# Pair-wise token mixing, two more pairs turned by the DMA crossbar behind held loads, and a shorter mask chain, in a block-sparse attention and mixer kernel on one core

## The chip, the cores and the metric

The kernel runs on one core of a Trainium2 chip. The metric is the device time of one execution in microseconds; the figure for a kernel is the median over its runs. Profiles come from one profiled execution, whose span (first to last instruction of the program) is a little shorter than its time.

The engines are named as in the profile: PE is TensorE (PEld its weight loads), DVE VectorE, ACT ScalarE, POOL GpSimd, SP the engine that issues most of the stores and the crossbar transposes.

## The reference

Inputs are q, k and v of shape (4 batches, 8 heads, 768 rows, 64), a table of three sampled key blocks for each of the 24 query blocks (a block is 32 rows), and four mixer weights. All arrays but the table are float32; the output is (4, 768, 512) in float32.

```python
scores = (q @ k.transpose(0, 1, 3, 2)) / np.sqrt(64)
# a key block is allowed when it neighbours the query block (distance <= 1),
# when either block is the first or the last, or when it is sampled for that query block
scores = np.where(mask, scores, -1e9)
attn = softmax(scores)
x = (attn @ v).transpose(0, 2, 1, 3).reshape(4, 768, 512)

h  = np.maximum(x.transpose(0, 2, 1) @ w_tok1, 0) @ w_tok2     # 768 -> 256 -> 768, over the rows
u  = x + h.transpose(0, 2, 1)
out = u + np.maximum(u @ w_ch1, 0) @ w_ch2                     # 512 -> 1536 -> 512, over the channels
```

## The kernel before

**Units of work.** Two heads make a pair; there are 16 pairs (`p`), four to a batch (`b`). The scores of a pair are made in nine visits (`t`, `jj`), each of four matmuls into one PSUM tile `ps`: 256 keys by 256 queries for both heads. ACT takes the exponential of a visit (`et`, L686), and PE multiplies `et` by v (`po`, L762, eight matmuls of 65 columns; column 65 sums the weights). DVE divides (L776, L777) and writes `x` of the batch, which the mixer reads.

**The mask.** For pairs 0 to 3 the mask goes into the score matmul as 24 more contraction rows (88 rows instead of 64), for one head at a time. For pairs 4 to 15 the two heads of a pair lie in the two halves of the contraction rows (64 rows each), two matmuls run side by side, and DVE multiplies `et` by a 0/1 mask (L694). Such visits go to PE two at a time. The rows of the mask are made at the start by a chain of small DVE operations (L353 to L375) from three GpSimd iotas and the sampled table; a matmul `pm_e` (L410) and copies (L417) bring them into `qtb[0]`.

**Turning k and q.** The score matmul needs k and q with the head dimension on partitions (`ktb`, `qtb`, four buffers each, pair p in buffer p % 4). For pairs below `NPE = 8`, PE turns them against an identity matrix (L618, `tk` and `tq`, 12 matmuls a pair) and DVE or ACT copies the result out of PSUM (L632, L647). From pair 8 on, SP issues two DMA transposes a pair (L587, the crossbar), from `klay` and `qlay`, which a DVE copy (L565) fills. The copies of these pairs are planned after the last load has landed (`all_loaded`).

**The loads.** k, q and v of a pair, as bfloat16, are three DMAs of GpSimd (L254); the queue goes on in the order of `loads`: pairs 4 to 15, with the channel weights (L273, L280) after pairs 5 and 7 and parts of the mask copies (L532) after pairs 5 to 7. A load waits for a free home (`homes`, which include unused halves of `ktb` and `qtb`).

**The mixer.** Token mixing of a batch is `tok(b, g)`, for the two halves `g` (two pairs each): 12 matmuls of 256 columns (`pm_tok`, L842), a ReLU (`a_t`), 12 of 256 columns (L867), and three DVE additions into `x` (L875). The result must be turned for the channel mixing (`uT`): for batch 0 on PE (`pm_ut`, L896, 12 matmuls for each half), for the others by SP's crossbar (L820). Channel mixing of a batch, `ch(b)`, is 24 groups of four matmuls of 384 columns (L934) with ReLUs on ACT or DVE (L804, L806), and then 6 groups of 12 matmuls of 512 columns (L960), DVE additions (L972) and stores by SP.

**The order.** A planner in the kernel's Python writes out the order of every engine's instructions ahead of time. It holds streams of PE work by priority (0 for scores, 1 for `po`, 2 for turning pairs, 0.5 for token mixing of batch 0, 3 for that of the others, 4 for channel mixing), a cost for each piece, due times for loads, and the number of buffers (`ps` 2, `pm` 3, `et` 7). At each planned moment the stream with the smallest number that is ready goes. ACT takes other work only when no exponential is pending. On the chip each engine then works strictly in this order, and waits where data is not there.

One detail of that order: the first channel matmuls of a group ask only for their own part of `uT`,

```python
yield 162.5, [st[b]["uT_there"][dmc], ch1_there[dmc]], tags, emit, ...
```

so that two of the four matmuls of the first group stand in PE's program as soon as half `g = 0` is mixed, and hold one of the three `pm` buffers until half `g = 1` is done.

Of the kernel before, what the change touches and what calls it, by code (L numbers as in the profile page):

```python
# [174 lines left out]
def kernel(  # L175
# [22 lines left out]
    NET = 7  # L198
    NPE = 8
    NT0 = 4  # L200
# [25 lines left out]
    def landing(issue, nbytes):  # L226
        dma["free"] = max(dma["free"], issue + 3.2 * US) + nbytes / RATE
        return Ev(dma["free"] + 0.15 * US)

# [31 lines left out]
    def load_tok(t):  # L261
        nc.gpsimd.dma_start(
            out=w_tok1[:, :, :], in_=APx(moe_w_tok1, 0, [[NC * DT, 128], [1, NC * DT]])
        )
        tok1_there.t = landing(t, S * DT * 2).t
        nc.gpsimd.dma_start(
            out=w_tok2[:, :, :, :], in_=APx(moe_w_tok2, 0, [[S, 128], [128 * S, 2], [1, S]])
        )
        tok2_raw.t = landing(t, S * DT * 2).t
# [50 lines left out]

    for i in range(8):
        idle_mm()
    nc.gpsimd.iota(dki[R, :], pattern=[[1, 24]], base=0, channel_multiplier=-1)
    nc.gpsimd.iota(qbi[R, :], pattern=[[0, 1]], base=0, channel_multiplier=1)
# [26 lines left out]
    t2add = sb1.tile([128, 24], BF16, name="t2add")  # L351

    nc.vector.tensor_copy(out=dkf[R, :], in_=dki[R, :])  # L353
    nc.vector.tensor_copy(out=edge[R, :], in_=qbi[R, :])
    nc.vector.tensor_tensor(out=dkf[R, :], in0=dkf[R, :], in1=dkf[R, :], op=ALU.mult)
    nc.vector.tensor_scalar(
        out=edge[R, :], in0=edge[R, :], scalar1=-11.5, scalar2=None, op0=ALU.add
    )
    nc.vector.tensor_tensor(out=edge[R, :], in0=edge[R, :], in1=edge[R, :], op=ALU.mult)
    nc.vector.tensor_scalar(  # L360
        out=edge[R, :], in0=edge[R, :], scalar1=121.0, scalar2=None, op0=ALU.is_gt
    )
    nc.vector.tensor_scalar(
        out=bandg[R, :], in0=dkf[R, :], scalar1=1.0, scalar2=edge[R, 0:1],
        op0=ALU.is_le, op1=ALU.max,
# [50 lines left out]
    def e2_copy(copy, hf, hd, t):  # L416
        copy(out=qtb[0][R, hd, 384 * hf : 384 * hf + 384], in_=t[R, 0:384])  # L417
# [3 lines left out]
    qt0 = first_turn("q", 0)  # L421
    first_lay(acopy, "k", 0)
    kt0 = first_turn("k", 0)
    e2a, e2b = e2_mm(0, psM, "pm"), e2_mm(0, psO, "po")
    for i in range(4):
        idle_mm()
    first_evac(acopy, "q", 0, 0, qt0)
    first_evac(acopy, "q", 0, 1, qt0)
    e2_copy(acopy, 0, 0, e2a)
    first_evac(vcopy, "k", 0, 0, kt0)  # L430
    first_evac(vcopy, "k", 0, 1, kt0)
    e2_copy(vcopy, 0, 1, e2b)
    first_lay(acopy, "k", 1)
    first_lay(vcopy, "q", 1)
    START = 6.3 * US
    P.now = START
    for eng in P.free_at:
        P.free_at[eng] = START
    P.free_at["dve"] = START + 550.0
    f_there = {("k", 0): Ev(START), ("q", 0): Ev(START), ("k", 1): Ev(), ("q", 1): Ev()}  # L440

# [109 lines left out]
    copied = {}  # L551
    all_loaded = Ev()

    def relayout(p):
        lays = {}
        for nm in ("k", "q", "v") if p else ("v",):
# [18 lines left out]
            if nm != "v" and p >= NPE:  # L575
                deps.append(all_loaded)
            lays[nm + "ev"] = P.op(("dve",), {"dve": 320.0}, deps, emit, prio=2 if nm != "v" else 3)
# [76 lines left out]
    def alias(a, b):  # L654
        a.same_as = b
# [48 lines left out]
    def qk_deps(p, t, jj):  # L704
# [4 lines left out]
        return deps + [rows_there[0]] * (t > 0)  # L709

    def qk_stream():
        todo = list(steps)
        while todo:
# [12 lines left out]

            s2 = todo.pop(0)
            yield lambda p=s2[0]: (p, 1) in qT_there
            evs = [Ev(), Ev()], [Ev(), Ev()]

            def emit(s=s, s2=s2, evs=evs):
                scores(s, evs[0][0], evs[1][0])
                scores(s2, evs[0][1], evs[1][1])
                evs[0][0].t = P.now + 330.0 + P.PE_LAT + P.SEM
                evs[0][1].t = P.now + 560.0 + P.PE_LAT + P.SEM

            yield 650.0, qk_deps(*s) + qk_deps(*s2), [("ps", 2), ("et", 2)], emit, None
            for x, ev in zip((s, s2), evs[0]):
                if x[1:] == (2, 2):
                    alias(qk_done[x[0]], ev)  # L740

# [54 lines left out]

    st = {}

# [31 lines left out]
    def tok(b, g):  # L830
        deps = [x_there[2 * g + 4 * b + i, h] for i in range(2) for h in range(3)] + [tok1_there]

        urgent = 0.5 if b == 0 else 3
        box = {}
# [18 lines left out]
        a_t = sbw.tile([128, 2, 256], BF16, tag="a_t", name=f"a_t{b}_{g}")  # L853
        a_there = relu_op(lambda: a_t[:, :, :], box["pm"][:, :, :], [last], urgent)
        alias(rel, a_there)
        u_evs = []
        for s2 in range(3):
# [21 lines left out]

            ev = P.op(("dve",), {"dve": 695.0}, [last], add, prio=urgent)  # L880
            alias(rel, ev)
            u_evs.append(ev)
        alias(a_rel, last)
        if b > 0:
            turn_by_crossbar(b, g, u_evs)
            return
        for dmc in (2 * g, 2 * g + 1):
            last, rel, tbox = Ev(), Ev(), {}
            for sc in range(NC):
                def emit(sc=sc, dmc=dmc, rel=rel, tbox=tbox):  # L890
                    if sc == 0:
                        if dmc == 0:
                            new_uT(b)
                        P.take("pm", rel)
                        tbox["pt"] = psM.tile([128, NC, 128], BF16, tag="pm", name=f"pm_ut_{b}_{dmc}")
# [4 lines left out]
                    )  # L900
                tags = [("pm", 1)] if sc == 0 else []
                if sc == 0 and dmc == 0:
                    tags.append(("uT", 1))
                yield 56.0, [u_evs[sc // 2]], tags, emit, last if sc == NC - 1 else None

# [6 lines left out]

            ev = P.op(("dve", "act"), {"dve": 555.0, "act": 740.0}, [last], evac, prio=urgent)
            alias(rel, ev)
            alias(st[b]["uT_there"][dmc], ev)

    def ch(b, pool, tag):
# [4 lines left out]
        for cc in range(12):  # L922
            for sh in range(2):
                last, rel, pbox = Ev(), Ev(), {}
                for dmc in range(4):
# [14 lines left out]
                    if first and cc == 0 and sh == 0:  # L940
                        tags.append(("rc", 1))
                    yield 162.5, [st[b]["uT_there"][dmc], ch1_there[dmc]], tags, emit, last if dmc == 3 else None
                ev = relu_op(
# [9 lines left out]
        for sc, lo, n in parts:  # L953
# [12 lines left out]
            def fin(eng, sc=sc, lo=lo, n=n, pbox=pbox):  # L966
# [10 lines left out]
                else:  # L977
# [4 lines left out]
                    )  # L982
                nc.sync.dma_start(
                    out=APx(out, b * S * DM + sc * DM + lo, [[NC * DM, 128], [1, n]]),
                    in_=o[:, 0:n],
                )

# [11 lines left out]

    def tok_stream(bs):  # L1000
        for b in bs:
            for g in range(2):
                yield from tok(b, g)

    def ch_stream():
# [5 lines left out]
    P.stream(2, tr_stream())  # L1011
    P.stream(0.5, tok_stream((0,)))
    P.stream(3, tok_stream((1, 2, 3)))
    P.stream(4, ch_stream())
    P.stream(1.8, mask_stream())


    loads = deque()
    for p in range(4, NP):
# [5 lines left out]
        if 5 <= p <= 7:  # L1025
            loads.append(spread_mask(p - 5))


# [9 lines left out]
    def pull():  # L1038
        while loads:
            x = loads[0]  # L1040
            if callable(x):
                if maskb_there.t is None:
                    return
                x(max(P.now, maskb_there.t))
            else:
# [6 lines left out]
                t, home = min(free_from)  # L1052
                load_pair(x, t, home)
                tenant[home] = x
                if x == NP - 1:
                    all_loaded.t = arrive["v", x].t
            loads.popleft()
# [36 lines left out]
```

The softmax here doesn't subtract the row's maximum and nothing guards it: scores larger than these inputs give would overflow.

## Time and profile before

| | |
|---|---|
| median of 7 runs (lowest to highest) | 257.35 us (256.69 to 257.98) |
| profiled execution: time, span | 256.69 us, 254.8 us |
| PE busy | 247.4 us, 2738 matmuls in the records |
| DVE busy | 180.3 us |
| ACT busy | 173.9 us, 139.0 of it in 144 exponentials |
| POOL busy | 49.1 us |
| DMA | 26.35 MB, 103 GB/s on average |
| exponentials of pair 0, pair 4, pair 8, pair 15 begin at | 7.42, 43.83, 94.78, 180.60 us |

The profiled execution is the fastest of the seven and lies 0.66 us under the median; 1.89 us of it lie outside the span. Busy times of PE count each matmul from its issue to its modelled end, so a chain of short matmuls reads as one busy stretch; what PE really spends is read from the distance between starts. Some matmul records are missing from the trace (2738 of 2757).

### The profile page before, as it was taken

To read this page: it belongs to the slowest core of one execution; us is meant where nothing else is said; L and a number is where in the kernel's file an instruction comes from. 1 tells how busy PE (TensorE), PEld (TensorE's weight loads), DVE (VectorE), ACT (ScalarE), POOL (GpSimd) and SP (SyncE) were. 2 spreads that over 40 slices of the span, in tenths; PEclk is the share of its full clock that TensorE was granted. 3 is DMA by queue.
4 is the path that set the end of the run, shared out by engine and by line. 5 is a ranking of instruction groups with operands and counts; after the bars stand their busy time and mean duration, and the time that the engine had idled before them with its cause. 6 is when DMAs were issued, how large, how long until landed. Compare 5 with 4: busy or idle time off the path is not lost.

```text
span 254.8 us, 6559 instructions
## 1 busy us (share of the span) xinstructions
PE 247.4 (97%) x2738; PEld 158.8 (62%) x2757; DVE 180.3 (71%) x397; ACT 173.9 (68%) x215; POOL 49.1 (19%) x84
## 2 busy tenths in 40 slices
PE   8899999999999999999999999999999999999995
PEld 3588888766566557555666566557567744565444
DVE  7987678898899889889989898988986313200222
ACT  5899999988787677678888767767776510277100
POOL 8846969477300000000000000000000000000000
PEclk9999999999999999999999999999999999999999
DMA  6999999999976342294043311411610222300122
GB/s 154 189 216 202 212 202 206 204 201 201 202 130 102 74 115 73 59 151 106 0 59 68 64 42 26 122 44 41 59 46 4 43 63 84 124 0 3 41 110 96
DMA packets 42461, 26.35 MB, mean 103 GB/s; under 512 B 23680, under 2 KB 38800, under 8 KB 42432
## 3 DMA queue, kind: packets, MB, share of 16 engines
q0 software_dynamic: 15104, 12.98, 32.1%
q1 hardware_dynamic: 27056, 12.76, 21.4%
q8 instruction: 21, 0.34, 0.5%
q10 hardware_dynamic: 272, 0.20, 0.3%
q14 instruction: 8, 0.07, 0.1%
HBM read 26.74 MB, written 6.29 MB: 130 GB/s over the span
## 4 chain that ended last, share of the span: by engine, by line
PE 88%; ACT 6%; DVE 3%; issue 2%; ACTq 0%
PE pm_ch L934 25%; PE pm_ch L960 24%; PE ps L676 15%; PE po L762 12%; ACT et L686 6%; PE pm_tok L867 4%; PE pm_tok L842 4%; PE ps_idle L316 2%; DVE x L875 1%; DVE et L694 1%; PE pm_ut L896 1%; DVE qtb L417 0%; PE tk L618 0%; PE pm_e L410 0%; PE tq L618 0%
## 5 line engine op out<-in xcount | busy, mean ns | idle before, releaser
L686 ACT ACTIVATE et<-ps 128x1024 bf16<-128x1024 f32 x144 | 139.0, 1024 | 33.1 <-PE ps L676 32.6
L934 PE MATMUL pm_ch<-uT,w_ch 128*128 128x384 bf16 x384 | 73.3, 326 | 0.1
L694 DVE TENSOR_TENSOR et<-et,mask 128x1024 bf16<-128x1024 bf16 x108 | 70.0, 684 | 1.7 <-ACT et L686 1.7
L960 PE MATMUL pm_ch<-w_ch,rc 128*128 128x512 bf16 (+2 forms) x293 | 68.3, 362 | 1.2 <-issue 0.3
L762 PEld LDWEIGHTS <-et 128*128 128x128 bf16 x1152 | 48.5, 97 | 17.7 <-issue 2.4
L676 PE MATMUL ps<-qtb,ktb 64*128 64x256 bf16 (+1 forms) x576 | 54.7, 272 | 1.3 <-ACT et L686 0.9
L762 PE MATMUL po<-vaug,et 128*128 128x65 bf16 x1152 | 54.9, 193 | 0.4 <-DVE x L777 0.2
L934 PEld LDWEIGHTS <-w_ch 128*128 128x128 bf16 x384 | 34.0, 97 | 20.9 <-issue 3.1
L972 DVE TENSOR_TENSOR o<-pm_ch,x 128x512 f32<-128x512 f32 x23 | 15.8, 687 | 41.0 <-PE pm_ch L960 41.0
L804 ACT ACTIVATE rc<-pm_ch 128x384 bf16<-128x384 f32 x56 | 27.5, 491 | 24.9 <-PE pm_ch L934 24.6
L676 PEld LDWEIGHTS <-ktb 64*128 64x128 bf16 (+1 forms) x576 | 29.3, 95 | 20.6 <-issue 15.6
L960 PEld LDWEIGHTS <-rc 128*128 128x128 bf16 x312 | 26.8, 97 | 24.1 <-issue 2.5
L806 DVE TENSOR_SCALAR rc<-pm_ch 128x384 bf16<-128x384 f32 x40 | 22.0, 555 | 5.7 <-PE pm_ch L934 5.0
L777 DVE TENSOR_TENSOR x<-po,recip 128x256 bf16<-128x256 f32 x48 | 20.4, 425 | 1.7
L875 DVE TENSOR_TENSOR x<-pm_tok,x 128x512 bf16<-128x512 f32 x24 | 16.0, 686 | 2.7 <-PE pm_tok L867 2.6
L776 DVE RECIPROCAL recip<-po 128x4 f32<-128x4 f32 x48 | 8.7, 181 | 12.9 <-PE po L762 12.4
L867 PE MATMUL pm_tok<-a_t,w_tok 128*128 128x256 bf16 x96 | 13.5, 275 | 0.1
L842 PE MATMUL pm_tok<-x,w_tok 128*128 128x256 bf16 x96 | 12.5, 273 | 0.0
L867 PEld LDWEIGHTS <-w_tok 128*128 128x128 bf16 x96 | 10.3, 127 | 1.6 <-issue 0.8
L842 PEld LDWEIGHTS <-w_tok 128*128 128x128 bf16 x96 | 8.9, 98 | 1.9 <-issue 0.8
L254 POOL DMA_DIRECT2D vraw<-in_v_dram x10 | 7.4, 739 | 2.4 <-DVE vaug L562 0.9
L532 POOL COPY mask<-maskb 128x240 bf16<-128x240 bf16 (+1 forms) x18 | 7.3, 482 | 0.0
(96 smaller groups left out, 114.9 us busy)
## 6 DMA issues: line engine op xcount, KB each, us to landing
out_dram<-o SPq DMA_DIRECT2D x23, 256.0 KB, 2.2
w_ch<-in_moe_w_ch_dram POOLq DMA_DIRECT2D x8, 384.0 KB, 10.3
vraw<-in_v_dram POOLq DMA_DIRECT2D x10, 192.0 KB, 7.6
kraw<-in_k_dram POOLq DMA_DIRECT2D x9, 192.0 KB, 9.4
qraw<-in_q_dram POOLq DMA_DIRECT2D x9, 192.0 KB, 7.9
w_tok<-in_moe_w_tok_dram POOLq DMA_DIRECT2D x2, 384.0 KB, 9.4
ktb<-in_v_dram POOLq DMA_DIRECT2D x3, 192.0 KB, 7.3
kf<-in_k_dram SPq DMA_DIRECT2D x2, 192.0 KB, 3.1
```

The lines of the kernel that those rows point to most:

```text
L676: nc.tensor.matmul(out=ps[:, hd, 256 * i : 256 * i + 256], lhsT=ktb[n][rows, h, 256 * jj + 128 * i : 256 * jj + 128 * i + 128], rhs=qtb[n] ...
L686: nc.scalar.activation(out=et[:, :, :], in_=ps[:, :, :], func=AF.Exp, scale=0.125)
L694: nc.vector.tensor_tensor(out=ets[s][:, :, :].rearrange("k h (i q) -> k h i q", i=2), in0=ets[s][:, :, :].rearrange("k h (i q) -> k h i q" ...
L762: nc.tensor.matmul(out=po[:, hd, c, :], lhsT=et[:, hd, 256 * i + 128 * c : 256 * i + 128 * c + 128], rhs=va[:, hd, 2 * jj + i, 0:65], star ...
L777: nc.vector.tensor_tensor(out=free(xs[b][:, pb // 2, 2 * t, 128 * (pb % 2) : 128 * (pb % 2) + 128], 0, [[64, 2], [256, 2], [1, 64]],), in0 ...
L804: nc.scalar.activation(out=o(), in_=i, func=AF.Relu)
L806: nc.vector.tensor_scalar(out=o(), in0=i, scalar1=0.0, scalar2=None, op0=ALU.max)
L842: nc.tensor.matmul(out=box["pm"][:, t, :], lhsT=w_tok1[:, sc, 128 * t : 128 * t + 128], rhs=xs[b][:, g, sc, :], start=(t == 0 and sc == 0) ...
L867: nc.tensor.matmul(out=ubox["pm"][:, i, :], lhsT=w_tok2[:, t, :, 2 * s2 + i], rhs=a_t[:, t, :], start=(i == 0 and t == 0), stop=(i == 1 an ...
L875: nc.vector.tensor_tensor(out=st[b]["u"][:, g, 2 * s2 : 2 * s2 + 2, :], in0=ubox["pm"][:, :, :], in1=xs[b][:, g, 2 * s2 : 2 * s2 + 2, :], ...
L934: nc.tensor.matmul(out=pbox["pm"][:, 0:384], lhsT=w_ch1[:, dmc, 128 * cc : 128 * cc + 128], rhs=st[b]["uT"][:, dmc // 2, 3 * sh : 3 * sh + ...
L960: nc.tensor.matmul(out=pbox["pm"][:, 0:n], lhsT=box["rc"][:, cc, 128 * sc : 128 * sc + 128], rhs=w_ch2[:, cc, lo : lo + n], start=(cc == 0 ...
```

## The change

1. The crossbar turns pairs 6 and 7 too (`NPE = 6`), so PE and the copies out of PSUM do that for pairs 1 to 5 only. So that these transposes meet few loads, GpSimd's queue is held: at four places (`GATES`) it reads one element of `ktb` and `qtb` of a turned pair before it issues more loads (before those of pairs 8, 13, 14 and 15 it waits for the turned pairs 7, 9, 10 and 11). The planner puts the copies of pairs 6 and 7 behind the estimated end of the loads before the first gate, those of pairs 8 to 15 behind that before the second (`quiet`).
2. Token mixing of batch 0 goes pair by pair (`tok_pair`): 12 + 12 matmuls of 128 columns, a ReLU, two additions, 6 turning matmuls a pair. Pairs 0 to 2 have priority 1.7, pair 3 has 0.5. Half `(1, 1)` of token mixing is now turned on PE, not by the crossbar.
3. The first matmul of a channel group waits for all four parts of `uT`.
4. Score visits of pairs from 4 on go one at a time until batch 0 is mixed; only then by twos.
5. At the start: the squares of the two mask terms are gone from the DVE chain (a bitwise AND on integers, and a product fused with the comparison), seven instead of eight idle matmuls, and the order of `pm_e` and its copy moves ahead of the turning of k.
6. The six stores of batch 0 are split in halves. Some of the planner's estimates change.

```diff
-    NPE = 8
+    NPE = 6
+    GATES = {7: 7, 9: 12, 10: 13, 11: 14}
...
-        return Ev(dma["free"] + 0.15 * US)
+        return Ev(dma["free"] + 1.3 * US)
...
-    for i in range(8):
+    for i in range(7):
         idle_mm()
-    nc.gpsimd.iota(dki[R, :], pattern=[[1, 24]], base=0, channel_multiplier=-1)
+    nc.gpsimd.iota(dki[R, :], pattern=[[1, 24]], base=33, channel_multiplier=-1)
...
+    nc.vector.tensor_scalar(
+        out=dki[R, :], in0=dki[R, :], scalar1=31, scalar2=None, op0=ALU.bitwise_and
+    )
     nc.vector.tensor_copy(out=dkf[R, :], in_=dki[R, :])
     nc.vector.tensor_copy(out=edge[R, :], in_=qbi[R, :])
-    nc.vector.tensor_tensor(out=dkf[R, :], in0=dkf[R, :], in1=dkf[R, :], op=ALU.mult)
...
-    nc.vector.tensor_tensor(out=edge[R, :], in0=edge[R, :], in1=edge[R, :], op=ALU.mult)
     nc.vector.tensor_scalar(
-        out=edge[R, :], in0=edge[R, :], scalar1=121.0, scalar2=None, op0=ALU.is_gt
+        out=edge[R, :], in0=edge[R, :], scalar1=edge[R, 0:1], scalar2=121.0,
+        op0=ALU.mult, op1=ALU.is_gt,
     )
...
+    e2a, e2b = e2_mm(0, psM, "pm"), e2_mm(0, psO, "po")
     kt0 = first_turn("k", 0)
-    e2a, e2b = e2_mm(0, psM, "pm"), e2_mm(0, psO, "po")
...
     e2_copy(acopy, 0, 0, e2a)
+    e2_copy(vcopy, 0, 1, e2b)
     first_evac(vcopy, "k", 0, 0, kt0)
     first_evac(vcopy, "k", 0, 1, kt0)
-    e2_copy(vcopy, 0, 1, e2b)
...
-                deps.append(all_loaded)
+                deps.append(quiet[int(p >= NV + 4)])
...
+            visit = [s]
+            if todo and (todo[0][1:] != (0, 0) or (todo[0][0], 1) in qT_there) and mixing():
+                visit.append(todo.pop(0))
...
-        if b > 0:
+        if (b, g) != (1, 1):
             turn_by_crossbar(b, g, u_evs)
             return
...
+    def tok_pair(p):
+        g, cols = p // 2, slice(128 * (p % 2), 128 * (p % 2) + 128)
+        urgent = 0.5 if p == 3 else 1.5
...
+                    nc.tensor.matmul(
+                        out=box["pm"][:, t, :], lhsT=w_tok1[:, sc, 128 * t : 128 * t + 128],
+                        rhs=xs[0][:, g, sc, cols],
+                        start=(t == 0 and sc == 0), stop=(t == 1 and sc == NC - 1),
+                    )
...
+        a_there = relu_op(lambda: a_t[:, :, 0:128], box["pm"][:, :, :], [last], urgent)
...
+                        nc.tensor.matmul(
+                            out=ubox["pm"][:, i, :], lhsT=w_tok2[:, t, :, 3 * s3 + i],
+                            rhs=a_t[:, t, 0:128], start=(i == 0 and t == 0), stop=(i == 2 and t == 1),
+                        )
...
+                nc.vector.tensor_tensor(
+                    out=xs[0][:, g, 3 * s3 : 3 * s3 + 3, cols], in0=ubox["pm"][:, :, :],
+                    in1=xs[0][:, g, 3 * s3 : 3 * s3 + 3, cols], op=ALU.add,
+                )
...
+                nc.tensor.matmul(
+                    out=tbox["pt"][:, sc, :], lhsT=xs[0][:, g, sc, cols],
+                    rhs=ident[:, :], start=(sc == 0), stop=(sc == NC - 1), is_transpose=True,
+                )
...
-                    yield 162.5, [st[b]["uT_there"][dmc], ch1_there[dmc]], tags, emit, last if dmc == 3 else None
+                    deps = st[b]["uT_there"] + ch1_there if first else []
+                    yield 162.5, deps, tags, emit, last if dmc == 3 else None
...
+                half = n // 2 if b == 0 else n
+                for at in range(0, n, half):
...
-    P.stream(0.5, tok_stream((0,)))
-    P.stream(3, tok_stream((1, 2, 3)))
+    P.stream(1.7, first_tok_stream((0, 1, 2)))
+    P.stream(0.5, first_tok_stream((3,)))
+    P.stream(3, tok_stream())
...
+    def gate(p):
+        for i, buf in enumerate((ktb, qtb)):
+            nc.gpsimd.tensor_copy(out=seen[0:1, i : i + 1], in_=buf[p % NV][0:1, 0, 0:1])
+        gate_t["t"] = qT_there[p, 1].t
...
+            if isinstance(x, tuple):
+                still = [e for e in quiet if e.t is None]
+                if still and x not in gates_seen:
+                    still[0].t = dma["free"] + 2.0 * US
+                    gates_seen.append(x)
+                if (x[1], 1) not in qT_there or qT_there[x[1], 1].t is None:
+                    return
+                gate(x[1])
```

## The prediction

> **What bounds the kernel now.** I read the page's busy times and chain first, then a table by stage, then PE's and ACT's timelines in the stage up to 54 us, then DVE's at the start. The page:
>
> ```profile
> PE 247.4 (97%) x2738; PEld 158.8 (62%) x2757; DVE 180.3 (71%) x397; ACT 173.9 (68%) x215; POOL 49.1 (19%) x84
> ...
> PE 88%; ACT 6%; DVE 3%; issue 2%; ACTq 0%
> ```
>
> PE is busy almost throughout, and the chain that ended last runs over PE for 88% of the span. The 6% on ACT are exponentials; the list of the chain's pieces puts nearly all of them before 47 us. A table by stage cuts the span at the first score matmul (6.8) and where channel mixing begins to run (54.2); after the stretch come its length, then the busy times of PE, PEld, DVE, ACT and POOL:
>
> ```profile
> 6.80:54.20 47.40, 45.52 (x693) 37.74 (x692) 38.50 (x95) 44.53 (x50) 34.07 (x58) 1.00 1.24 205
> 54.20:200.00 145.80, 144.67 (x1738) 91.27 (x1753) 126.53 (x264) 110.13 (x129) 9.19 (x13) 1.00 0.45 82
> 200.00:254.80 54.80, 51.40 (x291) 27.60 (x292) 9.92 (x17) 15.19 (x31) 0.00 (x0) 1.00 0.19 65
> ```
>
> The first row is the stage that the change rebuilds: PE and ACT are both nearly full there, and DVE has 9 us free. From 54.2 on PE has channel matmuls to fall back on and hardly idles. So the end of the program is: start, plus all of PE's work, plus what PE waits. For PE's work I need distances between starts, from PE's timeline (start, length of the merged stretch, group):
>
> ```profile
> 42.44 0.50 PE L618 MATMUL tk<-ident,klay 128*128 128x128 bf16 x6
> 42.78 0.50 PE L618 MATMUL tq<-ident,qlay 128*128 128x128 bf16 x6
> 43.21 0.61 PE L676 MATMUL ps<-qtb,ktb 64*128 64x256 bf16 x8
> 43.75 0.90 PE L762 MATMUL po<-vaug,et 128*128 128x65 bf16 x24
> ...
> 46.18 1.48 PE L842 MATMUL pm_tok<-x,w_tok 128*128 128x256 bf16 x12
> 47.50 1.12 PE L762 MATMUL po<-vaug,et 128*128 128x65 bf16 x24
> ```
>
> A turning matmul of 128 columns costs (42.78 - 42.44) / 6 = 0.056 us, a token matmul of 256 columns 1.32 / 12 = 0.110. Going from 128 to 64 rows costs 0.43 - 6 x 0.056 = 0.095, and the eight score matmuls plus the way back cost 0.54: two by two at 0.109 a pair of them 0.44, and 0.10 for the return. The 24 `po` matmuls at 43.75 run on to the next group at 44.49, so a visit of eight is 0.74 / 3 = 0.245. A visit of 88 rows is 0.44 in the chain.
>
> **PE's work in the rebuilt stage.** Counted in the order of the built programs, from the first score matmul to the first channel group that runs. Before: 36 visits of 88 rows (15.8), 10 of 64 rows (2.2), 10 changes of row mode (0.95), 42 `po` visits (10.3), 48 token matmuls (5.3), 114 turning matmuls (6.4), mask and two early channel matmuls (0.9): 41.9 of 47.4 us, so PE waits 5.5. After: 36 (15.8) and 8 visits (1.8), 16 changes (1.5), 37 `po` visits (9.1), 96 narrow token matmuls at 0.056 (5.4), 90 turning matmuls (5.0), 0.6: 39.2.
>
> **PE's work in all**, behind the first score matmul: 24 turning matmuls of pairs 6 and 7 go (-1.34), 12 for half (1, 1) come (+0.67), token mixing +0.10 (96 x 0.056 for 48 x 0.110), eight more changes of row mode because eight visits stand alone (+0.76). Sum +0.2 us: this change does not save PE work. It can gain only at the start and in what PE waits.
>
> The narrow token matmuls have no row of their own. The 128-column turning matmuls say 0.056. The weight loads of the second token step take 127 ns (L867) against 97 for others, since their columns are strided; behind 97 ns loads `po` keeps a distance of 0.03, so 30 ns more allow 0.06. The 256-column step with the same loads holds 0.110, which is the upper end: 48 x 0.054 = +2.6 us. I take 0.056.
>
> [...]
>
> **What PE waits.** In the rebuilt stage ACT sets the pace. Its timeline:
>
> ```profile
> 48.14 0.69 ACT L804 ACTIVATE a_t<-pm_tok 128x512 bf16<-128x512 f32 x1
> 49.04 1.94 ACT L686 ACTIVATE et<-ps 128x1024 bf16<-128x1024 f32 x2 [0.21 <-PE ps L676]
> 51.54 1.94 ACT L686 ACTIVATE et<-ps 128x1024 bf16<-128x1024 f32 x2 [0.56 <-PE ps L676]
> 53.36 0.81 ACT L909 COPY uT<-pm_ut 128x768 bf16<-128x768 bf16 x1
> ```
>
> Exponentials start 0.92 apart when they follow on; the ReLU at 48.14 takes 0.90 of that pace, each of the copies at 43.15, 45.65 and 53.36 takes 0.68. From the first exponential (7.42) to 54.2, 44 exponentials (40.5) and four such operations (2.9) make 43.4 of 46.8 us; ACT waits 3.4. The stage ends when pair 3 is mixed, and that mixing is late: it begins after pair 3, half a batch at a time, and its hand-overs through DVE leave PE standing (PE's timeline):
>
> ```profile
> 50.01 0.41 PE L762 MATMUL po<-vaug,et 128*128 128x65 bf16 x8
> 50.51 0.60 PE L867 MATMUL pm_tok<-a_t,w_tok 128*128 128x256 bf16 x4
> ```
>
> Eight `po` are 0.245, but 0.50 lie between 50.01 and 50.51. Four such holes up to 54.3 (also before 52.31, 52.91 and 54.22) come to 0.26 + 0.25 + 0.14 + 0.20 = 0.85 us. After the change three of four pairs are mixed between earlier visits, channel mixing may begin after 44 instead of 46 visits, and of ACT's four other operations one is left (a copy of `tk`). With 42 exponentials (38.6), one copy (0.7) and the same 3.4 us of waits the stage lasts 42.7 on ACT. DVE's 38 us of work leave it room. With a start 0.25 earlier it ends at 7.17 + 42.7 = 49.9; PE stands at 49.9 - 6.55 = 43.35 with 39.2 of work, waits 4.15 instead of 5.5, and that is -1.35.
>
> **The start.** DVE's chain, from its timeline:
>
> ```profile
> 1.33 0.86 DVE L355 TENSOR_TENSOR dkf<-dkf 24x24 f32<-24x24 f32 x1
> 2.12 0.14 DVE L356 TENSOR_SCALAR edge<-edge 24x1 f32<-24x1 f32 x1
> 2.29 0.80 DVE L359 TENSOR_TENSOR edge<-edge 24x1 f32<-24x1 f32 x1
> ```
>
> GpSimd's two selects (L326, L330) run from 1.30 to 2.16 and from 2.23 to 3.09, and both squares end with them, though one has a single column; the one-tensor operation between takes 0.14. They go (-1.66), an AND comes (+0.15). But the three L371 operations, two tensors each and 0.23 apiece, move up beside the second select, and may be held to its end at 3.09. Then the mask sum ends near 4.2 instead of 4.98. The first score also needs k: its layout copy ends at 4.65, set by its load, and DVE's copies of the turned k (0.74) now come after one copy of `pm_e` (0.56), so it can start at 6.3 to 6.6. Bounds of the gain: 0 and 0.5; I take 0.25. The idle matmul removed (0.43 apart at that point) lies under that.
>
> **Held loads.** Before, load 8 is issued at 41.3; now GpSimd first waits for pair 7's transposes. Those stand behind the third mask product of pair 4, about 47 us; four at 1.3 us on SP and 2.9 to landing give 55. Fifteen loads at 0.98 apart end near 72. Pair 8 starts at 94.8 and its copies stand after pair 6: some 15 us of cover, and the transposes of pairs 6 and 7 have 10 before pair 6 starts at 67.3. Gates 13, 14 and 15 have similar room. GpSimd's queue holds only loads then, SP's only later transposes and stores; if the cover were gone, DVE's copies of pair 8 would wait, with mask products and ReLUs, and so PE, queued behind. I cost this, the half stores and the eight reads at nothing. The first transpose of before, issued at 71.89 with the last loads still landing, took 7.3 us against the median of 2.9; held loads avoid that, but nobody waited.
>
> **Sum.** +0.2 - 1.35 - 0.25 = -1.4 us: 256.69 becomes 255.3 for the profiled execution, which lies 0.66 under the median; so 255.9 as a median.
>
> **Rivals.** *Nothing is gained* (257.3): in the rebuilt stage PE's work per pair rises to 8.4 us (7.2 to 7.7 before, in pairs 1 and 2), as much as nine exponentials (8.3). Two queues in fixed order, both full, wait for each other, and what is saved after pair 3 is lost in pairs 1 to 3. For it: pair 3, with 8.8 of work, took 10.1 us. Against it: 30 to 40 us, where half 0 is mixed between visits, has almost no holes on PE.
> *Slower* (258.6): the hand-overs of pairs 0 to 2 cost what the late half cost, 0.85 each, 2.6 in all; -1.4 + 2.6 = +1.2. It decides from 0.55 to 0.7 a pair. For it: five steps a pair instead of a half batch, each waiting in order on DVE with scores queued behind. Against: the mixing of half 0 had next to none.
> *Much faster* (253.7): ACT waits only in pair 0 (1.2 of the 3.4), a further 2.2.
> *The hold bites*: only if pair 7's transposes landed 15 us later than reckoned; 260 or more.
>
> **How the numbers follow.** Forecast 0.45 (own range 254.7 to 256.9), nothing gained 0.22, slower 0.16, much faster 0.13, the hold or the strided loads at their upper end 0.04. The measurement can tell about 0.3% (0.8 us) from no change. Faster by that: nearly all of the forecast and the much faster case, 0.56; within it 0.23; slower 0.21. The range runs from the much faster case to just over the slower one: 253.7 to 259.0.
>
> **What would show it.** Right: channel mixing runs from 49 to 51 us; ACT's first 44 exponentials have one other operation among them; narrow token matmuls 56 to 60 ns apart; DVE's wait-free chain gives `t2add` near 4.2; the last transposes of pair 7 land near 55 and no DVE copy of pair 8 waits. Wrong: channel mixing after 52, holes of 0.2 us before each `pm_tok` and `pm_ut` step, or PE idle from 60 to 110 us.

## The result and the profile after

The changed kernel takes 261.13 us in the median of 25 runs (258.72 to 265.13), the kernel before 257.35 us of 62. The ratio is 1.0103, with an interval of 1.0082 to 1.0124: slower, where 255.9 us and faster had been forecast. All comparisons leave the most disturbed runs out; medians and lowest to highest here are of all runs of a kernel. The profiled execution took 259.1 us with a span of 257.3.

The page of the changed kernel, its busy times, its granted clock in 40 slices, and its chain:

```profile
PE 246.8 (96%) x2773; PEld 159.7 (62%) x2792; DVE 177.4 (69%) x395; ACT 175.1 (68%) x218; POOL 51.9 (20%) x92
...
PEclk9999999999999999799999999999999999999999
...
PE 80%; DMA 8%; POOL 4%; DVE 2%; issue 1%; ACT 1%; SPq 1%; POOLq 0%; DVEq 0%
```

Before, the chain that ended last had PE with 88% and no DMA. Now 8% are DMA and 4% POOL (about half of that DMA share is one load of k from 9.8 to 21.0 us, the rest crossbar transposes at 88 to 102 us), and one slice near 105 us has less than the full clock. PE's busy time is about what it was, so the time is not in the amount of PE's work. The table by stage (length, then busy PE, PEld, DVE, ACT, POOL, granted clock, DMA share, GB/s) finds it:

```profile
6.80:50.00 43.20, 40.97 (x664) 34.97 (x663) 32.29 (x85) 41.64 (x44) 26.58 (x46) 1.00 1.18 196
50.00:100.00 50.00, 49.44 (x602) 31.16 (x608) 43.65 (x97) 39.78 (x48) 15.16 (x25) 1.00 0.94 133
100.00:103.20 3.20, 0.87 (x10) 0.38 (x9) 1.43 (x5) 1.94 (x2) 2.67 (x6) 0.97 1.11 244
103.20:106.60 3.40, 3.40 (x27) 2.35 (x27) 2.40 (x4) 0.00 (x0) 1.64 (x3) 0.53 1.28 227
106.60:200.00 93.40, 92.87 (x1146) 58.82 (x1153) 81.04 (x166) 71.84 (x86) 0.00 (x0) 1.00 0.29 58
```

Everywhere but in two rows PE is nearly full. From 100 to 103.2 it works 0.87 us, and in the 3.4 us behind that its granted clock is 0.53. PE's timeline in these rows, and then DVE's:

```profile
100.44 0.39 PE L1045 MATMUL pm_ch<-w_ch,rc 128*128 128x512 bf16 x1
103.16 1.65 PE L876 MATMUL pm_tok<-a_t,w_tok 128*128 128x256 bf16 x7 [2.33 <-DVE a_t L817]
```

```profile
98.79 0.36 DVE L569 COPY qlay<-qtb 128x768 bf16<-128x768 bf16 x1 [1.21 <-DMA qtb<-qlay]
...
101.39 0.36 DVE L569 COPY klay<-kraw 128x768 bf16<-128x768 bf16 x1 [1.37 <-DMA ktb<-klay]
102.15 0.36 DVE L569 COPY qlay<-qraw 128x768 bf16<-128x768 bf16 x1 [0.40 <-DMA qtb<-qlay]
102.42 0.68 DVE L817 TENSOR_SCALAR a_t<-pm_tok 128x512 bf16<-128x512 f32 x1
```

PE waits for the ReLU `a_t`. On DVE that ReLU stands behind the layout copies of pairs 12 and 13; they write `klay` and `qlay`, which are two deep, so each waits until the transpose of the pair two before, 10 or 11, has read its buffer. Why those are late stands in SP's and GpSimd's rows:

```profile
92.13 1.22 SPq L591 DMA_TRANSPOSE qtb<-qlay  x1
93.51 1.55 SPq L591 DMA_TRANSPOSE ktb<-klay  x1
95.17 1.54 SPq L591 DMA_TRANSPOSE qtb<-qlay  x1
```

```profile
91.00 0.21 POOL L1129 COPY seen<-qtb 1x1 bf16<-1x1 bf16 x1 [2.12 <-DMA qtb<-qlay]
91.45 0.72 POOL L255 DMA_DIRECT2D kraw<-in_k_dram  x1 [0.25 <-issue]
...
98.81 0.37 POOL L1129 COPY seen<-qtb 1x1 bf16<-1x1 bf16 x1 [5.05 <-DMA qtb<-qlay]
```

The gate on pair 9 opens at 91.0 and releases load 13 just as pairs 10 and 11 are being transposed. The last DMA piece of the chain there is "95.17 6.88 DMA qtb<-qlay": 6.88 us from issue to landing, where pair 9's last transpose, issued at 88.12 ahead of these loads, took 2.73 ("88.12 2.73 DMA qtb<-qlay"). The hole (2.5 us between starts: 103.16 - 100.44, less the 0.22 of one matmul of 512 columns) and what is lost in the 3.4 us at a clock of 0.53 (1.6) make some 4.1 us; 257.3 - 4.1 = 253.2 us, about the span that had been forecast (255.3 less 1.9).

### The profile page after: what moved, and what is told of

It is laid out like the page before. It is cut to its first block, busy times and chain, and to the rows that moved or that the text cites. A ratio compares the mean times of both kernels' runs of the same rounds, so it can differ in the third digit from the quotient of the medians.

```text
span 257.3 us, 6656 instructions
## 1 busy us (share of the span) xinstructions
PE 246.8 (96%) x2773; PEld 159.7 (62%) x2792; DVE 177.4 (69%) x395; ACT 175.1 (68%) x218; POOL 51.9 (20%) x92
## 4 chain that ended last, share of the span: by engine, by line
PE 80%; DMA 8%; POOL 4%; DVE 2%; issue 1%; ACT 1%; SPq 1%; POOLq 0%; DVEq 0%
PE pm_ch L1018 25%; PE pm_ch L1045 21%; PE ps L680 13%; PE po L774 13%; DMA kraw<-in_k_dram 4%; DMA qtb<-qlay 4%; PE pm_tok L876 4%; PE pm_tok L851 3%; ACT et L690 1%; POOL vraw L255 1%; PE pm_tok_p L961 1%; POOL kraw L255 1%; DVE et L698 1%; POOL qraw L255 1%; PE pm_tok_p L938 1%
## 5 line engine op out<-in xcount | busy, mean ns | idle before, releaser
L1045 PE MATMUL pm_ch<-w_ch,rc 128*128 128x512 bf16 (+2 forms) x293 | 67.2, 363 | 0.9 <-issue 0.2
L774 PEld LDWEIGHTS <-et 128*128 128x128 bf16 x1152 | 50.0, 98 | 18.4 <-issue 4.6
L774 PE MATMUL po<-vaug,et 128*128 128x65 bf16 x1152 | 57.0, 194 | 0.7 <-ACT et L690 0.4
L815 ACT ACTIVATE rc<-pm_ch 128x384 bf16<-128x384 f32 x60 | 29.5, 492 | 25.7 <-PE pm_ch L1018 25.3
L817 DVE TENSOR_SCALAR rc<-pm_ch 128x384 bf16<-128x384 f32 x36 | 19.8, 555 | 6.2 <-PE pm_ch L1018 5.3
L876 PE MATMUL pm_tok<-a_t,w_tok 128*128 128x256 bf16 x72 | 11.6, 292 | 2.5 <-DVE a_t L817 2.3
L884 DVE TENSOR_TENSOR x<-pm_tok,x 128x512 bf16<-128x512 f32 x18 | 11.9, 684 | 1.9 <-PE pm_tok L876 1.8
L876 PEld LDWEIGHTS <-w_tok 128*128 128x128 bf16 x72 | 7.7, 130 | 4.4 <-issue 4.0
L851 PE MATMUL pm_tok<-x,w_tok 128*128 128x256 bf16 x72 | 9.7, 273 | 0.0
L1129 POOL COPY seen<-ktb 1x1 bf16<-1x1 bf16 x4 | 0.9, 214 | 33.2 <-DMA ktb<-klay 33.2
```

The source lines that it names most:

```text
L774: nc.tensor.matmul(out=po[:, hd, c, :], lhsT=et[:, hd, 256 * i + 128 * c : 256 * i + 128 * c + 128], rhs=va[:, hd, 2 * jj + i, 0:65], star ...
L815: nc.scalar.activation(out=o(), in_=i, func=AF.Relu)
L817: nc.vector.tensor_scalar(out=o(), in0=i, scalar1=0.0, scalar2=None, op0=ALU.max)
L851: nc.tensor.matmul(out=box["pm"][:, t, :], lhsT=w_tok1[:, sc, 128 * t : 128 * t + 128], rhs=xs[b][:, g, sc, :], start=(t == 0 and sc == 0) ...
L876: nc.tensor.matmul(out=ubox["pm"][:, i, :], lhsT=w_tok2[:, t, :, 2 * s2 + i], rhs=a_t[:, t, :], start=(i == 0 and t == 0), stop=(i == 1 an ...
L1045: nc.tensor.matmul(out=pbox["pm"][:, 0:n], lhsT=box["rc"][:, cc, 128 * sc : 128 * sc + 128], rhs=w_ch2[:, cc, lo : lo + n], start=(cc == 0 ...
```

## The experiments

Medians beside the kernel before on the same chip (257.6 to 257.8 us). Unless a text says otherwise, every kernel computes all of the reference.

**Third layout buffers** (`e1`): 

```diff
-  lay = sbw.tile([128, NC, 2, D], BF16, tag=f"{nm}lay", bufs=2, ...)
+  lay = sbw.tile([128, NC, 2, D], BF16, tag=f"{nm}lay", bufs=3, ...)
```

(The small last stores take their tiles from tag "o", to make room.)

> A third buffer for klay and qlay (the last three small stores share the buffers of the others, to make room); every engine's order stays that of the changed kernel. Theory 1 (DVE's queue: the copies of pairs 12 and 13 wait for a buffer that the transposes of pairs 10 and 11 still read, and the ReLU a_t and so PE stand behind them): the waits at 98.8, 101.4 and 102.2 us go, except for what the load of pair 13 still lacks (under 1 us); the 2.5 us hole on PE at 100.7 and the slow stretch after it go, 3 to 4.5 us less than the changed kernel: 256 to 257.5. Rival 2 (the late load of pair 13 itself holds DVE): the hole shrinks by less than 1 us, 260 and more. Rival 3 (the rest of the change costs time): no difference, 261.

256.70 us (255.03 to 261.35), ratio 0.9949 (0.9917 to 0.9981). DVE's timeline of this kernel no longer has a wait for a transpose at that place:

```profile
98.91 0.35 DVE L569 COPY klay<-kraw 128x768 bf16<-128x768 bf16 x1
99.25 0.36 DVE L569 COPY qlay<-qraw 128x768 bf16<-128x768 bf16 x1
99.86 0.69 DVE L817 TENSOR_SCALAR a_t<-pm_tok 128x512 bf16<-128x512 f32 x1 [0.25 <-PE pm_tok L851]
```

The transposes themselves are as late as in the changed kernel (7.0 us for the one issued at 95.32; the median of all ten of q is 3.6, in the changed kernel 3.8): the third buffer only keeps DVE from waiting for them. Its profiled execution took 255.25 us: 1.44 less than that of before, against 1.4 forecast; over the runs the gain is 0.5%, some 1.3 us.

**The copies planned later** (`e2`; the planner's estimate for a transpose raised):

```diff
-  ev = P.op(("sp",), {"sp": 900.0}, deps, emit, prio=1, lat=5000.0)
+  ev = P.op(("sp",), {"sp": 900.0}, deps, emit, prio=1, lat=7000.0)
```

> The planner reckons 7 us instead of 5 from a transpose to its landing, and so puts DVE's copies of pairs 12 and 13 behind the ReLU a_t and one more mask product; buffers, loads and gates stay. Theory 1: PE's hole at 100 us goes or falls under 0.5 us, 256 to 257.5. Rival 2: the copies still hold DVE, and with it mask products of pair 8, so a hole of 2 us stands some 3 us later, 259 to 261. Rival 3: 261.

260.01 us (255.98 to 264.38), ratio 0.9993 (0.9955 to 1.003). In the profile (257.3 us) `a_t` comes at 101.09, ahead of the copies, and PE has no hole at 100 us; but other waits take its place at 110 to 120 us, and over the runs little is gained. As a cure it failed; as evidence it says only that `a_t` was late because of its place behind the copies.

**No second hold** (`e3`):

```diff
-    GATES = {7: 7, 9: 12, 10: 13, 11: 14}
+    GATES = {7: 7, 9: 15}
```

> GpSimd reads crossbar output only before the load of pair 8; pairs 13 to 15 are loaded straight after pair 12. Theory 1 with its cause upstream (the loads released at 91 us run beside the transposes of pairs 10 and 11, which then land after 6 to 7 us instead of 3): loads end near 86, these transposes land in 3 us, no hole at 100: 255.5 to 257.5. Rival 4 (transposes are as slow here for another reason, such as the stores on the same queue): they still take 6 us and DVE still waits, 259 to 261.

256.84 us (255.43 to 261.17), ratio 0.9947 (0.992 to 0.9975). The reads of pair 9 stand behind the last load in the queue here, so they hold nothing: loads 8 to 15 go out in one row after the first gate. No hole at 100 us. Since the planner puts the copies of pairs 8 on behind the last load, these pairs are also turned later (in `e15`, with the same gates, pair 8's first transpose goes out at 89.80 us, in the changed kernel at 81.77), so the edit moves the transposes as well as the loads. Three runs lay at 261, and the profiled execution was one of those. More on it below.

**Token mixing and start without the crossbar's part** (`e4`): `NPE = 8`, `GATES = {}`, and the copies planned behind the last load as before.

> The changed kernel with PE turning pairs 1 to 7 as before, all copies for the crossbar behind the last load, and no gates. Theory 1: no hole at 100 us; against the changed kernel 24 more turning matmuls (1.3 us) and no hole: 256 to 257.3, between nothing and 1.3 us faster than the kernel before. Rival 3 (pair-wise mixing, single visits or the half stores cost time): 258 and more.

257.12 us (255.71 to 261.29), ratio 0.9961 (0.9932 to 0.9989): without held loads the rest of the change gains.

**The crossbar's part alone** (`e8`): the kernel before with `NPE = 6`, the gates and `quiet`; and the same with third layout buffers (`e11`).

> The kernel before with only the crossbar's part of the change: pairs 6 and 7 are turned by the crossbar and the loads are held twice; token mixing, mask chain and first order as before. Computes the same. Theory of the held loads: loads 13 to 15 are released beside the transposes of pairs 10 and 11, these land in 6 to 7 us instead of 2.8, and the layout copies of pairs 12 and 13 wait for that; the planner puts other work behind these copies than in the changed kernel, so PE's hole may be shorter: 0 to 4 us, against 0.3 to 1.3 us of turning work saved: 257 to 260. Rival, the crossbar's part is sound and the loss needs the new token mixing: 256 to 257, no wait on DVE above 1 us near 100 us.

> The kernel before with only the crossbar's part of the change, and third layout buffers for k and q. Computes the same. Theory of the held loads: without the wait of the layout copies for the transposes of pairs 10 and 11 the loss of the crossbar's part alone (263.1, hole on PE of 4.7 us) is gone and the saved turning work remains: 256 to 257.5. Rival, the loss comes from the late loads themselves and not from the buffers: still over 259.

Alone: 263.12 us (258.44 to 267.25), ratio 1.0105 (1.0052 to 1.0159). DVE's and PE's timelines:

```profile
99.77 0.36 DVE L566 COPY qlay<-qraw 128x768 bf16<-128x768 bf16 x1 [5.44 <-DMA qtb<-qlay]
```

```profile
101.39 0.62 PE L763 MATMUL po<-vaug,et 128*128 128x65 bf16 x8 [4.67 <-DVE et L695]
```

The same kind of copy waits for the same kind of transpose, here with mask products behind it. The loss needs nothing of the new token mixing. With third buffers: 257.42 us (256.11 to 263.32), ratio 0.9979 (0.9955 to 1.0002); no hole, and no measurable gain either.

**Whole stores** (`e12`):

```diff
-                half = n // 2 if b == 0 else n
+                half = n
```

> The changed kernel with the stores of the first batch whole again instead of in halves. Computes the same. Theory: two half stores hold SP for 1.0 us, one whole for 0.5, ahead of the transposes of pairs 9 to 11; with whole stores these are issued 0.5 to 1 us earlier, but so is the release of loads 13 to 15, which they wait beside; the hole of 2.5 us at 100 us shrinks by 0 to 1 us: median 260 to 261. Rival, the half stores are what delays them: hole gone, 257.

261.25 us (259.94 to 264.15; six runs), hole 3.1 us, now at 104 to 107. The hole grew instead of shrinking by up to 1 us, so that part of the expectation missed; the half stores are not the cause.

**PE's clock at the start.** After this the changed kernel still spread from 258.7 to 265 us. A clue lies in its first rows beside those of the kernel without the second hold: PE's timeline of the changed kernel, then of `e3` (261.17 us).

```profile
5.17 1.03 PE L317 MATMUL ps_idle<-one 128*128 128x512 bf16 x4
...
7.59 1.24 PE L680 MATMUL ps<-qtb,ktb 88*128 88x256 bf16 x8
```

```profile
5.61 1.91 PE L317 MATMUL ps_idle<-one 128*128 128x512 bf16 x4
...
9.37 1.89 PE L680 MATMUL ps<-qtb,ktb 88*128 88x256 bf16 x8
```

The same four idle matmuls take twice as long, and in `e3` that goes on to 20 us (channel mixing then runs from 55.3 us, from 49.96 in `e1`), though the table by stage gives a granted clock of 1.00 there: the clock records of this trace begin only at 20.1 us, and a stretch without a record counts as full clock. The distances show what the records leave out: the score matmuls at 18.44 are 0.21 us apart, those at 20.05 0.12. The records of the changed kernel begin at 4.0 us, those of `e4` at 5.0 and of `e2` at 9.8 (the 8.7 in the expectation of `e5` below is too early: `e2`'s score matmuls are still 0.213 us apart at 9.55 and 0.109 from 9.89). With one idle matmul less and the mask chain's end at 4.51, PE stands for some 0.3 us before `pm_e`; before, it did not stand at all. Five runs on that:

```diff
     qt0 = first_turn("q", 0)
+    idle_mm()                     # e5, e6, e10, e14
...
-    for i in range(7):
+    for i in range(8):            # e10, e14 (four instead in e13)
         idle_mm()
```

`e5` is the changed kernel with the one idle matmul in the hole, `e6` that with third buffers, `e10` with third buffers and nine idle matmuls, `e14` the changed kernel with nine, `e13` with third buffers and four.

> The changed kernel with one idle matmul of 512 columns more, between the turning of the first half of q and the first mask product, where its PE stood from 4.28 to 4.57 us. Computes the same. In the profiles of a few runs so far PE works at half rate (an idle matmul every 0.427 us instead of 0.216) up to 4.0, 5.0, 8.7 or 20 us, and the later the slower the run. Theory of the clock at the start: the hole decides it; with it filled PE reaches its full rate by 9 us in every execution, the runs of 263.8 to 265.1 vanish, the fastest stay at 258.8 to 259.3 (the mask product is 0.13 later), median 261.1 to about 259.4. The hole at 100 us stays (2.5 us), since nothing is done about it. Rival, the spread has another source (loads that land late at the start): same spread, median 261.

> The changed kernel with both cures: a third layout buffer each for k and q, and the idle matmul in the hole at the start. Theory (two separate losses): no hole at 100 us, no cold start, 255.1 to 256.9 with the median near 255.6, about what was predicted for the change, and no run over 258.5. Rival, the spread has another source: as with the third buffers alone, 256.7, with some runs of 259 to 261.

> The changed kernel with third layout buffers, the idle matmul in the hole and an eighth one at the head. Computes the same. Theory of the clock at the start: each executed idle matmul makes an early rise of the clock likelier, at 0.43 us of later start while cold: fastest runs 255.6 to 256.1, fewer runs above 257 than the five in twelve at 256.9 to 257.5 with one idle matmul in the hole; median 256. Rival: nothing but later: 257.4, same spread.

> The changed kernel with third layout buffers and four idle matmuls at the head instead of seven. Computes the same. Theory of the clock at the start: PE stands from 2.7 us to the turning at 3.96 and is cold up to 8 us or later in most executions: no run under 256, most at 257 to 261, median 257.5 to 260. Rival, the idle matmuls decide nothing: as with seven, fastest 255.0 to 255.5, median 256.7.

> The changed kernel itself, its layout buffers two deep, with nine idle matmuls before the mask product (eight at the head, one in the hole). Computes the same. Theory of two separate losses: the hole at 100 us stays with its half clock, so the fastest runs are at 259 to 260 and the median at 259.5 to 260; no run above 262, where the changed kernel had nine of 26. Rival, the spread of the changed kernel comes from the hole at 100 us: runs of 263 to 265 again.

| kernel | median, lowest to highest | ratio to before |
|---|---|---|
| `e5` hole filled | 259.84 (259.17 to 261.83) | 1.0085 (1.0056 to 1.0114) |
| `e6` third buffers, hole filled | 257.08 (255.53 to 260.84) | 0.9948 (0.9914 to 0.9982) |
| `e10` third buffers, nine idle | 255.82 (255.09 to 258.7) | 0.9947 (0.9911 to 0.9983) |
| `e13` third buffers, four idle | 260.96 (257.16 to 263.55) | 1.0039 (0.9989 to 1.0089) |
| `e14` changed kernel, nine idle | 260.80 (259.37 to 265.72) | 1.0124 (1.0085 to 1.0162) |

With third buffers four, seven, eight and nine idle matmuls give 261.0, 256.7, 257.1 and 255.8, and ratios of 1.0039, 0.9949, 0.9948 and 0.9947. Between seven and nine no difference is shown. With four no run is under 257.16, where seven reach 255.03: what PE does before the first score can count. (Part of the 261.0 is the hole at 100 us, see below.) `e5` had no run above 261.83, but the nine of `e14` did not make the changed kernel's long runs go away (five of twelve above 262; in the changed kernel it was ten, not nine), and the expectation for `e14` missed. Where that spread comes from is not shown. The hole alone is not enough: three of those five runs have a granted clock of 0.979, and the one profile with that clock (`e12`, 262.53 us) has a clock of 0.50 from 10.5 to 17.4 us besides the hole.

The profile of `e13` shows why third buffers are no full cure. SP, GpSimd and DVE:

```profile
93.21 1.40 SPq L591 DMA_TRANSPOSE qtb<-qlay  x1
```

```profile
103.09 0.37 POOL L1129 COPY seen<-qtb 1x1 bf16<-1x1 bf16 x1 [8.56 <-DMA qtb<-qlay]
```

```profile
103.07 0.36 DVE L569 COPY qlay<-qraw 128x768 bf16<-128x768 bf16 x1 [2.80 <-DMA qtb<-qlay]
```

Pair 10's transpose, issued at 93.21 beside load 13, is seen at 103.07: 9.9 us. Even a buffer that is three deep is not free then, and the hole is back (2.2 us).

**The start on the kernel before, and the old start on the new kernel** (`e7`: seven idle matmuls instead of eight before; `e9`: third buffers, and the old idle matmuls, mask chain and first order).

> The kernel before with seven idle matmuls at the start instead of eight. Computes the same. Theory of the clock at the start: PE now stands for some 0.4 us until the mask sum is there at 4.98, so that in part of the executions it works at half rate up to 8.7 or 20 us; runs of 259 to 262 appear among those of 256.5 to 258, median 258 or more. Rival, one idle matmul does nothing: 257.4, up to 258.2.

> The changed kernel with third layout buffers for k and q, and with the start of the kernel before: eight idle matmuls, the squares in the mask chain, the first order. Computes the same. Theory of the clock at the start: the new start saves 0.25 us where PE gets warm early and costs where it doesn't; with the old start the fastest runs are at 255.3 to 255.8 (third buffers alone: 255.03 to 255.5), no run lies at 259 or above with a granted clock of 1.0, median 256 to 256.5. Rival, the spread of the third-buffer runs has nothing to do with the start: same spread as there, median 257.

`e7`: 258.08 us (256.63 to 260.51), ratio 1.0028 (0.9996 to 1.0061): in the expected direction, not beyond doubt. `e9`: 257.05 us (256.43 to 261.8), ratio 0.9983 (0.9957 to 1.0008), a miss: even its fastest run is 1.4 us above that of `e1`. The planner starts from other times here and writes another order, in which channel mixing runs from 53.2 instead of 49.9. So this run doesn't isolate the start.

**Neither late loads nor a cold start** (`e15`, `e16`): `GATES = {7: 7, 9: 15}` and nine idle matmuls, layout buffers two deep (`e15`) or three deep (`e16`). As in `e3`, the second gate holds no load, not even load 15 as the first text below has it.

> The changed kernel with loads 13 and 14 no longer held behind pairs 9 and 10 (one gate for load 15 is left, as in the run with one gate), and nine idle matmuls ahead of the mask product. Layout buffers two deep as in the change. Computes the same. Theory (the late loads beside the transposes of pairs 10 and 11 make the hole at 100 us and its half clock; the idle matmuls make the runs at 261 go): no hole near 100 us, runs at 255.4 to 257.3, none above 258.5, median 255.9. Rival, the third buffers were the cure and what is left of the spread is chance: runs of 258 to 261 in a third of the cases, median 257.

> As the run with one gate and nine idle matmuls, with third layout buffers as well. Computes the same. Theory: where no load lands beside the transposes of pairs 10 and 11 the third buffers have nothing left to hide: the same time within 0.3 us, 255.9, none above 258.5. Rival, the buffers carry the gain: at least 0.7 us faster than without them.

`e15`: 256.44 us (255.84 to 256.89), ratio 0.9934 (0.991 to 0.9958), the narrowest of all, with every granted clock at 0.999 or 1.0. It beats both kernels, by 0.7% the one before. DVE, SP and the table by stage:

```profile
99.26 0.36 DVE L570 COPY qlay<-qraw 128x768 bf16<-128x768 bf16 x1 [0.23 <-DMA qtb<-qlay]
99.78 0.69 DVE L818 TENSOR_SCALAR a_t<-pm_tok 128x512 bf16<-128x512 f32 x1 [0.16 <-PE pm_tok L852]
```

```profile
94.76 1.29 SPq L592 DMA_TRANSPOSE qtb<-qlay  x1
96.15 2.60 SPq L1071 DMA_DIRECT2D out_dram<-o  x4
98.85 1.22 SPq L592 DMA_TRANSPOSE ktb<-klay  x1
100.17 1.23 SPq L592 DMA_TRANSPOSE qtb<-qlay  x1
```

```profile
100.00:106.60 6.60, 6.07 (x79) 3.90 (x79) 5.99 (x13) 4.37 (x6) 0.00 (x0) 1.00 0.62 119
```

The buffers are two deep as in the changed kernel, and the copy of pair 11 waits 0.23 us for the transpose of pair 9 two before it. The last load was issued at 81.11, ahead of all transposes of pairs 8 to 11 (89.80 to 102.88). Pair 10's two, issued at 98.85 and 100.17, land in 2.8 us each (the median of all ten of q is 2.9, in the changed kernel 3.8), though four stores on the same queue come just before them; that speaks against the stores (rival 4 of `e3`). Pair 9's last, issued at 94.76, is seen at 99.26, 4.5 us later; why is open. So the loads released beside the transposes are the cause, and the two buffers and DVE's order only carry it to PE. Two pairs of kernels say it, second hold or not: ratios of 1.0103 against 0.9947 with seven idle matmuls, 1.0124 against 0.9934 with nine, some 4 and 5 us. In both pairs the transposes move with the loads, as said at `e3`. `e16`: 257.32 us (256.63 to 259.9), ratio 0.9996 (0.996 to 1.0033), 0.9 slower than `e15` where the same time was expected. Five of its runs have a granted clock of 0.984 or 0.985, and the profiled one shows where:

```profile
14.00:16.00 2.00, 2.00 (x24) 1.75 (x22) 1.28 (x3) 1.02 (x1) 1.14 (x3) 0.50 1.15 246
```

The clock falls to a half from 10.9 to 17.7 us, behind PE's first waits for an exponential (the first 0.7 us long). The changed kernel's profile has the same wait, of 0.67 us, and no such fall, so what decides it is open. The other runs of `e16` are still some 0.6 us above those of `e15`; why is open too.

## Why the prediction was wrong

**The step that failed** is in "Held loads": "Gates 13, 14 and 15 have similar room ... I cost this, the half stores and the eight reads at nothing." The step looked at one side of a gate, who needs the loads behind it and when, and there it was right: nobody waited for load 13. It did not look at the other side, what is on the DMA engines at the moment when the gate opens. A gate that opens when pair 9 is turned opens while pairs 10 and 11 are being turned, since they follow at once. PE idle from 60 to 110 us, a sign of being wrong that the prediction had named, came at 100 us. The missing term was 4.1 us in the profiled execution, and some 4 to 5 us by the ratios of kernels with and without the second hold.

**A row misread.** The text did name a price for a transpose beside loads, 7.3 us for the first one of before, and dismissed it ("nobody waited"). That price is not a transpose's. The 7.3 is the longest entry in a view of everything that writes `ktb`, and there it belongs to loads of v into `ktb` (issued at 59.98 and 62.93, 7.3 us each). The transpose issued at 71.89 landed in 2.9 us, though the last load, issued at 65.87, landed only 7.3 us later, at about 73.2. So the trace of before had no slow transpose: it neither showed that held loads save anything, nor gave the price that the second hold then cost.

**The cover, named but not followed.** The text said what would queue behind late copies (mask products, ReLUs, and so PE), for pair 8. For pairs 12 and 13 exactly this happened, through the two layout buffers. "The hold bites" was priced at 260 or more and given 0.04, since it was tied to pair 7's transposes being 15 us late; GpSimd read them at 58.3 and 58.9 us where 55 was reckoned, and no copy of pair 8 waited. The rival had the right price and the wrong gate.

**What was right.** Channel mixing runs from 49.9, as forecast:

```profile
49.89 0.66 PE L1018 MATMUL pm_ch<-uT,w_ch 128*128 128x384 bf16 x3
```

From the first score matmul at 6.08 that is 43.8 us, with 39.2 counted as work: waits of 4.6 us where 4.15 were forecast and 5.5 there before. That the end falls on the forecast is in part luck: the first exponential came 0.16 us earlier than forecast, and the stage on ACT lasted 42.9 us from there where 42.7 were forecast. ACT's first 44 exponentials had one other operation among them, as forecast. The narrow token matmuls cost 0.056 us each, the lower end:

```profile
19.12 0.44 PE L938 MATMUL pm_tok_p<-x,w_tok 128*128 128x128 bf16 x5
19.40 0.60 PE L680 MATMUL ps<-qtb,ktb 88*128 88x256 bf16 x4
```

(19.40 - 19.12) / 5 = 0.056. The slower rival, 0.85 us of hand-overs for each of pairs 0 to 2, did not come: the stage ended when forecast.

**The start.** The first exponential came at 7.01 (7.17 forecast), the mask sum at 4.51 instead of 4.2, because a single-tensor cast also ended only with GpSimd's select (0.86 us for 24x24 elements in DVE's row "1.33 0.86 DVE L357 CAST dkf<-dki 24x24 f32<-24x24 int32 x1"; the select runs from 1.30 to 2.16). Whether "the idle matmul removed ... lies under that" holds is not settled. PE's clock rises at very different times in kernels with seven (4.0 us in the changed kernel, 20.1 in `e3`), but the kernel before with seven (`e7`) is not slower beyond doubt, and nine against seven gives ratios of 1.0124 against 1.0103, 0.9934 against 0.9947 and 0.9947 against 0.9949: a price is not shown.

**The sum.** With the failed step taken out, the total comes near the forecast of 1.4 us: 1.44 of gain in the profiled execution of `e1`, and 1.3 to 1.7 by the ratios of `e1`, `e3`, `e6`, `e10` and `e15`. That is the total only. `e4`, without the crossbar's part, gains some 1.0, and `e16`, with every cure, nothing. What stays open is how much of the spread up to 265 us comes from transposes that land still later than in the profile (9.9 us in `e13`), and how much from half-clock stretches in the first 20 us.

## What to carry to other kernels

A gate on transfers has two sides: besides asking who needs what is held, ask what is in flight when it opens, and put it where the queue that it protects is empty on both sides of it, as at the first gate here: when it opens at 59.3 us, the next transpose is over 20 us away. Before a price is read from a view of a tile, check which of its operations the number belongs to. A transfer's landing time belongs in the estimate at the value it has beside other traffic (here 6.9 us where 2.8 was the median), and from there follow the buffer that it reads, the engine that refills that buffer, and what is next in that engine's order. Here a stop of PE of 2.5 us cost some 4.1, since 3.4 us at a clock of 0.53 came behind it. Filler work ahead of the first real matmul can be part of the schedule (with third buffers, four idle matmuls gave 261.0 us where seven gave 256.7; part of the 261.0 is the hole at 100 us): look at when the clock rises before taking it away.

## What the runs showed of the hardware

- Crossbar transposes of k and q landed in 2.8 us (median of before); beside loads of GpSimd's queue the same transposes took 6.9 us in the changed kernel, and 9.9 in `e13` until one was seen. Without loads beside them some took up to 4.8 us (the one issued at 52.69 in the changed kernel).
- In the changed kernel, after PE stood for about 2.5 us from 100.7 on, its granted clock was 0.53 from 103.2 to 106.6.
- When PE reaches its full rate at the start differs from profile to profile: at 4.0 us (changed kernel), 5.0 (`e4`), 9.8 (`e2`) or 20 (`e3`). Ahead of that the idle matmuls start 0.43 us apart instead of 0.22. Stretches at half clock later on lasted 3.4 us (changed kernel) and 6.8 us (`e16`).
- The run of `e3` at half rate until 20 us has its channel mixing 5.4 us later than `e1` (55.32 against 49.96) and took 261.17 us, where the same kernel's fastest took 255.43; that is 2%.
